# Top-k attention and a gated feed-forward on one core: the first two batches in another order, and one full product for the left-over keys

## The chip, the core and the metric

The kernel runs on one core of a Trainium2 chip. Time is device time in microseconds (us), the median over runs of the whole kernel. The engines are called PE (TensorE, matrix products; PEld is its weight load), DVE (VectorE), ACT (ScalarE), POOL (GpSimd) and SP (SyncE, which only issues transfers here).

## What is computed

The reference has two blocks, one behind the other, all in float32.

```python
# attention: q, k, v are (8, 8, 576, 64): batch, head, position, dimension
scores = scale * np.matmul(q, k.transpose(0, 1, 3, 2))
kth = np.partition(scores, -top_k, axis=-1)[..., -top_k:-top_k + 1]   # top_k = 32
scores = np.where(scores >= kth, scores, -1000000000.0)
scores = scores - np.max(scores, axis=-1, keepdims=True)
attn = np.exp(scores)
attn = attn / (np.sum(attn, axis=-1, keepdims=True) + 1e-09)
attn_out = np.matmul(attn, v)
# feed-forward on (4608, 512): one row per batch and position, heads side by side
h = x @ w_in                                  # w_in (512, 2048)
g = h * np.clip(h + 3.0, 0.0, 6.0) / 6.0
out = g @ w_out                               # w_out (2048, 512)
```

## The kernel before

**Tiles.** The 576 positions of a head are 4 tiles of 128 and a rest of 64. Two heads make a `Pair`, which is loaded, transposed on PE and kept for the whole batch. A `Duo` is two pairs (four heads) for one query tile `qt`; two duos cover a tile of a batch. A duo with `qt == J` (J is 4) is a left-over duo: its 64 remaining queries of both heads of a pair share the 128 partitions, so that it has half the rows to search. Each batch has eight full and two left-over duos, 80 in all.

**A duo's work, in order.** `scores` makes the products on PE, and ACT copies them from PSUM to `sc`. `top` finds the 32nd largest score of a row on DVE: four rounds of MAX8 (L249) with MATCH_REPLACE8 (L253) between them, for pair 0 and then for pair 1. `shift` (POOL, L262 and L265) and `exp` (ACT, L272 to L282) make the masked exponentials and their sum; `inverse` (DVE, L286) is the reciprocal; `weights` (POOL) scales the rows (L296) and splits the words into 16-bit halves (L305); `flip` (L311) transposes them by a transfer that SP issues; `join` puts the halves together again (L317), for pair 0 on ACT and for pair 1 on POOL. `values` multiplies by v on PE (L337) into one PSUM tile `pv`, and ACT copies this to the tokens `xT`, or `xr` for left-over queries (L344). In `values`, the two heads of a pair are side by side as two tiles of 64 columns of the array: four products of 128 keys each from `vm`, and a fifth from `vr` for the 64 left-over keys of each head. `vr` has zeros where the other head's keys are, and both heads' left-over weights lie in the same tile `eT[:, J, :]`.

**The written-out order.** There is no automatic scheduling. The main loop goes through the duos `m`, with eight slots `i` each; slot number 8m + i. In each slot come one round of `top`, then `convert_step`, then `parts(slot)`, which emits the steps of earlier duos that are due, then `piece`, which emits feed-forward work. The tables `usual`, `early` (duos 0 and 1) and `soon` (the last two) say how many slots after its duo's first slot a step is due: in `usual`, `exp0` at 4, `inverse0` at 7, `join0` at 13, `values` at 20. Each engine works off its instructions in the order in which they were emitted.

**Weights.** `w_in` and `w_out` arrive as 64-bit numbers and are converted in 32 chunks, one per slot in the first duos: a load (L102), Abs and a scaled copy on ACT (L108, L111) with a clamp on POOL (L109), then two DVE operations (L117, L118), then an add on POOL (L122). `convert` is a generator; before, it yields once after the load and once after the first stage, and DVE's part comes two slots after ACT's.

**Feed-forward.** `feed_forward` works on a block of 128 or 256 tokens: products `h` (L361), ACT's relu and copy, the gate on POOL (L375, L376), products `acc` (L383), a scaled copy and the output. A 128-token block is 16 pieces and a 256-token block 32. The main loop emits some 3 to 9 pieces a duo, by how many are left. Blocks have 256 tokens (`two`) in batches 1 to 6 and 128 in batches 0 and 7; the left-over queries of two batches make one 128-token block in `xr`, of which there is one buffer. `xT` has two, so `values` first emits all that is left of the block that last used the buffer:

```python
if hp == 0 and c0 == 0:
    while len(blocks) > 1 and blocks[-2] in todo:
        piece()
    state["xT"] = xtpool.tile([P, NHP, 2 * P], F32, tag="xT", name="xT")
```

Of the kernel before, what the change touches and what calls it, by code (L numbers as in the profile page):

```python
# [29 lines left out]
def kernel(  # L30
# [9 lines left out]
    nc = tc.nc  # L40
    P = nc.NUM_PARTITIONS
    B, H, S, D = q.shape
    DM, FF = moe_w_in.shape
    J = S // P
# [51 lines left out]
    def convert(dst, src):  # L96

        st = kqpool.tile([P, 2 * WC], U32, tag="kq", name="st")
        nc.sync.dma_start(st[:], src)  # L102
        yield
        words = st[:].rearrange("p (n two) -> p n two", two=2)
        lo, hi = words[:, :, 0], words[:, :, 1]
        a = gpool.tile([P, WC], F32, tag="g", name="a")
        y = gpool.tile([P, WC], F32, tag="g", name="y")
        nc.scalar.activation(a[:], hi.bitcast(F32), AF.Abs)  # L108
        nc.gpsimd.tensor_scalar(a[:], a[:], HI_MOST, HI_LEAST, ALU.min, ALU.max)  # L109

        nc.scalar.activation(y[:], lo, AF.Copy, bias=2.0, scale=2.0**-51)  # L111
        yield

        au, yu = a[:].bitcast(U32), y[:].bitcast(U32)
        nc.vector.tensor_scalar(au, au, 3, None, ALU.logical_shift_left)  # L117
        nc.vector.scalar_tensor_tensor(  # L118
            out=yu, in0=hi, scalar=0x80000000, in1=yu,
            op0=ALU.bitwise_and, op1=ALU.bitwise_or,  # L120
        )
        nc.gpsimd.tensor_tensor(  # L122
            dst.bitcast(I32), a[:].bitcast(I32), y[:].bitcast(I32), ALU.add
        )
# [59 lines left out]
    class Duo:  # L184
# [4 lines left out]


        def __init__(self, pairs, qt):
            self.pairs, self.qt = pairs, qt
            self.rest = qt == J
            self.nt = 1 if self.rest else 2
            self.nb = J + 2 if self.rest else 2 * J + 1
            self.m, self.less = [None] * 2, [None] * 2
            self.e16, self.t16, self.eT = [None] * 2, [None] * 2, [None] * 2
# [115 lines left out]
        def join(self, u):  # L313

            eT = self.eT[u] = kqpool.tile([P, 2 * J + 1, P], F32, tag="kq", name="eT")
            copy = nc.gpsimd.tensor_copy if u else nc.scalar.copy
            copy(  # L317
                eT[:, 0 : self.nb, :]
                .rearrange("p c q -> p (c q)")
                .bitcast(U16)  # L320
                .rearrange("p (x h) -> p h x", h=2),
                self.t16[u][:, 0 : 2 * self.nb, :].rearrange("p (h c) q -> p h (c q)", h=2),
            )

        def values(self, dst):

            w = R if self.rest else P
            pv = ps_w.tile([P, 512], F32, tag="w", name="pv")
            for u in range(2):
                pr, eT = self.pairs[u], self.eT[u]  # L330
                for c in range(J + 1):
                    for hh in range(2):
                        if self.rest:
                            rhs = eT[:, c if c < J else J + hh, hh * R : (hh + 1) * R]
                        else:
                            rhs = eT[:, c if hh == 0 or c == J else J + 1 + c, :]
                        nc.tensor.matmul(  # L337
                            pv[hh * D : (hh + 1) * D, u * w : (u + 1) * w],
                            pr.vm[:, hh, c, :] if c < J else pr.vr[:, hh, :],
                            rhs,  # L340
                            start=(c == 0),
                            stop=(c == J),
                        )
            nc.scalar.copy(dst, pv[:, 0 : 2 * w].rearrange("p (u q) -> p u q", u=2))  # L344


# [55 lines left out]
    duos = []  # L402
    for b in range(B):
        halves = [pairs[b][0:2], pairs[b][2:4]]
        for qt in range(J):
            duos += [Duo(h, qt) for h in halves]

            if b == B - 1 and qt == 0:
                duos += [Duo(h, J) for h in halves]
            elif b < B - 1 and qt % 2 == 0:  # L410
                duos.append(Duo(halves[qt // 2], J))
    assert J == NHP == 4
    per_batch = 2 * J + 2
    ND = len(duos)
    todo = []
    blocks = []
    left = 0
# [2 lines left out]
    def piece(count=1):  # L420
        nonlocal left
        for _ in range(count):
            while todo:
                try:
                    gates.append(next(todo[0]))
                    left -= 1
                    break
                except StopIteration:
                    todo.pop(0)
            else:  # L430
                gates.append(None)
            if len(gates) > 2:
                gate = gates.pop(0)
                if gate:
                    gate()

    def queue(*block):
        nonlocal left
        todo.append(feed_forward(*block))
        if block[0] is not state.get("xr"):  # L440
            blocks.append(todo[-1])
        left += block[1] // 8

    state = {}

    def values(m):

        u = duos[m]
        b, qt, hp = u.pairs[0].b, u.qt, u.pairs[0].hp
        if u.rest:  # L450
            if b % 2 == 0 and hp == 0:
                state["xr"] = xrpool.tile([P, NHP, P], F32, tag="xr", name="xr")
            u.values(state["xr"][:, hp : hp + 2, (b % 2) * R : (b % 2 + 1) * R])
            if b % 2 == 1 and hp == 2:

                def rows(t0):
                    return [
                        (i * R, (i + 1) * R, out[(b - 1 + i) * S + JP : (b + i) * S, :])
                        for i in range(2)
                    ]  # L460

                queue(state["xr"], P, rows)
            return

        two = 0 < b < B - 1
        c0 = qt % 2 * P if two else 0
        if hp == 0 and c0 == 0:
            while len(blocks) > 1 and blocks[-2] in todo:
                piece()
            state["xT"] = xtpool.tile([P, NHP, 2 * P], F32, tag="xT", name="xT")  # L470
        u.values(state["xT"][:, hp : hp + 2, c0 : c0 + P])
        if hp == 2 and (not two or c0):

            def rows(t0):
                t = qt - c0 // P + t0 // P
                return [(0, P, out[b * S + t : b * S + JP : J, :])]

            queue(state["xT"], c0 + P, rows)
# [8 lines left out]
            next(c)  # L487
            landing.append(c)

    def convert_step(depth=2):  # L490

        if len(converting) >= depth or not landing:
            for c in converting[:1]:
                next(c, None)
            del converting[:1]
        if landing:
            c = landing.pop(0)
            next(c)
            converting.append(c)
        land()  # L500

    def pair_at(m, first):
# [23 lines left out]
        shift1=7, exp1=8, inverse1=11, weights1=12, flip1=14, join1=17, values=20,  # L526
    )
    early = dict(
        shift0=3, exp0=3, inverse0=4, weights0=4, flip0=6, join0=8,
        shift1=7, exp1=7, inverse1=8, weights1=8, flip1=10, join1=12, values=13,  # L530
    )
    soon = dict(
        shift0=3, exp0=3, inverse0=5, weights0=5, flip0=7, join0=10,
# [4 lines left out]
        for part, at in (early if m < 2 else soon if m >= ND - 2 else usual).items():  # L538
            queued.setdefault(8 * m + at, []).append((m, part))

    def parts(slot):
        for m, part in sorted(queued.get(slot, []), key=lambda x: x[1][:-1] != "shift"):
            if part == "values":
                values(m)
            else:
                getattr(duos[m], part[:-1])(int(part[-1]))

    for m in range(ND + 3):
        u = duos[m] if m < ND else None

        level = (left >= 8) + (left >= 16) + (left >= 48)
        count = ((3, 4, 4, 5) if u and u.rest else (6, 7, 8, 9))[level]
        for i in range(8):
            if u:
                u.top(i // 4, i % 4)
            convert_step()
            if m == 0 and i == 0:
                first[3].load()
            if m == 0 and i in (1, 2):
                first[i + 1].transpose()  # L560
            if i == (3 if m == 0 else 1) and m + 1 < ND:
                duos[m + 1].scores()
            parts(8 * m + i)
            if m == 0 and i in (1, 4):
                for p in duos[i // 4].pairs:
                    p.load_values()
            if i == 0:
                p = pair_at(m, 4)
                if p:
                    p.load()  # L570
            if i == 3 and u and u.pairs[0].b and 1 <= m % per_batch <= 2:
                for p in duos[m - 1].pairs:
                    p.load_values()
            if i == 5:
                p = pair_at(m, 5)
                if p:
                    p.transpose()
            piece((i + 1) * count // 8 - i * count // 8)
# [36 lines left out]
```

## Time and profile before

| | before |
|---|---|
| median of 3 runs | 1631.08 us (1630.5 to 1633.21) |
| span of the profiled run | 1631.0 us |
| PE busy | 1466.9 us (90%) |
| DVE busy | 1470.0 us (90%) |
| ACT busy | 1088.6 us (67%) |
| POOL busy | 1140.9 us (70%) |
| MAX8 (L249), 1152 of them | 614.5 + 202.9 us on DVE |
| MATCH_REPLACE8 (L253), 864 of them | 423.8 + 211.9 us on DVE |
| feed-forward on PE (L361, L383) | 472.5 + 517.9 us |
| values on PE (L337) | 169.1 us with `vm`, 62.5 us with `vr` |

A busy time counts an engine only while an instruction runs on it. Each float32 product appears as two records of PE. In the profile's lines, an arrow points from what is read to what is written; "x16" is a count; square brackets at the end of a timeline row give how long the engine was idle ahead of it, and on whom it waited. The chain is followed back from the last instruction to whatever released each step, so that it says which engine set the pace at which time. The rows of 40 digits cut the span into equal slices, each digit being the busy share in tenths.

### The profile page before, as it was taken

Reading aid. Unit: us, or ns where it says so; the run is one execution under the profiler, and the core shown is the slowest. Engines: PE = TensorE matmul, PEld = TensorE weight load, DVE = VectorE, ACT = ScalarE, POOL = GpSimd, SP = SyncE. Lnnn points to the kernel's source line nnn. Section 1 sums busy time; section 2 is a strip of 40 time slices with the busy share of each in tenths; the row PEclk is TensorE's granted clock in tenths of the full one; section 3 lists DMA queues with packets and bytes.
Section 4 is the critical chain, followed back from the end, with each engine's and each line's share of the span. In section 5 each row is a group of like instructions: output and inputs, shape, how many; then the busy total and the mean of one; then the engine's idle time right before and its main releaser. Section 6 shows DMA issues by size and latency. Waiting matters only on the chain.

```text
span 1631.0 us, 25648 instructions
## 1 busy us (share of the span) xinstructions
PE 1466.9 (90%) x8736; PEld 979.2 (60%) x8736; DVE 1470.0 (90%) x3105; ACT 1088.6 (67%) x1863; POOL 1140.9 (70%) x1266
## 2 busy tenths in 40 slices
PE   5147699848999999899999999898999999899999
PEld 2134467627567584756567584656577584657775
DVE  5999999999999989999999889999999889999500
ACT  5566677667777676767767676767767676757521
POOL 3787577757787776867787776867787775867741
PEclk9568799979999999999999999999999999999999
DMA  8553434444444434454344424454354424333410
GB/s 231 156 171 64 101 63 89 97 95 83 71 98 99 94 56 92 86 109 85 65 104 89 94 56 92 88 107 84 65 105 89 94 56 94 80 60 72 66 22 13
DMA packets 450307, 144.29 MB, mean 88 GB/s; under 512 B 433280, under 2 KB 441472, under 8 KB 450176
## 3 DMA queue, kind: packets, MB, share of 16 engines
q1 hardware_dynamic: 450176, 142.65, 42.3%
q8 instruction: 69, 1.13, 0.3%
q14 instruction: 62, 0.51, 0.1%
HBM read 45.09 MB, written 9.44 MB: 33 GB/s over the span
## 4 chain that ended last, share of the span: by engine, by line
DVE 48%; PE 43%; ACT 3%; POOL 3%; SPq 1%; issue 1%; DMA 0%; POOLq 0%; ACTq 0%
DVE m L249 25%; DVE wk L253 20%; PE acc L383 16%; PE h L361 15%; PE pv L337 5%; PE big L226 3%; DVE y L118 1%; POOL eT L317 1%; PE big L229 1%; ACT sc L277 1%; DVE a L117 1%; SPq L150 1%; POOL sc L296 1%; PE big L214 1%; SPq L154 1%
## 5 line engine op out<-in xcount | busy, mean ns | idle before, releaser
L249 DVE MAX8 m<-wk 128x8 f32<-128x576 f32 x864 | 614.5, 748 | 3.1
L383 PE MATMUL acc<-w_out,g 128*128 128x512 f32 x1152 | 517.9, 600 | 5.1 <-POOL g L376 5.1
L361 PE MATMUL h<-xT,w_in 128*128 128x256 f32 (+1 forms) x2560 | 472.5, 343 | 0.0
L361 PEld LDWEIGHTS h<-xT,w_in 128*128 128x128 f32 x2560 | 410.0, 194 | 48.4 <-issue 10.3
L253 DVE MATCH_REPLACE8 wk<-m,wk 128x576 f32<-128x576 f32 x576 | 423.8, 742 | 0.0
L383 PEld LDWEIGHTS acc<-w_out,g 128*128 128x128 f32 x1152 | 213.5, 191 | 244.6 <-issue 234.6
L305 POOL COPY e<-sc 128x2304 uint16<-128x2304 uint16 (+1 forms) x192 | 322.0, 1687 | 10.1
L337 PE MATMUL pv<-eT,vm 128*64 128x128 f32 (+1 forms) x2560 | 169.1, 278 | 119.3 <-POOL eT L317 84.8
L272 ACT ACTIVATE sc<-sc,m 128x576 f32<-128x576 f32 x288 | 209.7, 773 | 47.5 <-DVE m L249 47.1
L337 PEld LDWEIGHTS pv<-eT,vm 128*64 128x64 f32 x2560 | 138.2, 144 | 161.7 <-POOL eT L317 89.6
L277 ACT ACTIVATE sc<-sc,shift 128x576 f32<-128x576 f32 x288 | 219.8, 766 | 21.5 <-POOL shift L265 18.7
L296 POOL TENSOR_SCALAR sc<-sc,den 128x576 f32<-128x576 f32 x288 | 213.0, 750 | 27.6 <-DVE den L286 27.1
L262 POOL TENSOR_TENSOR shift<-m 128x2 f32<-128x2 f32 (+1 forms) x160 | 32.1, 201 | 269.7 <-DVE den L286 266.8
L317 POOL COPY eT<-t 128x2304 uint16<-128x2304 uint16 (+1 forms) x80 | 208.5, 2606 | 5.7 <-DMA t<-e 4.6
L253 DVE MATCH_REPLACE8 wk<-m,sc 128x576 f32<-128x576 f32 x288 | 211.9, 742 | 0.0
L317 ACT COPY eT<-t 128x2304 uint16<-128x2304 uint16 (+1 forms) x80 | 208.9, 2611 | 0.0
L249 DVE MAX8 m<-sc 128x8 f32<-128x576 f32 x288 | 202.9, 741 | 0.9 <-ACT sc L235 0.9
L376 POOL TENSOR_TENSOR g<-g,hs 128x512 f32<-128x512 f32 x144 | 183.7, 1276 | 12.0
L344 ACT COPY xT<-pv 128x256 f32<-128x256 f32 x64 | 23.8, 372 | 232.8 <-PE pv L337 232.8
L375 POOL TENSOR_SCALAR g<-g 128x512 f32<-128x512 f32 x144 | 88.6, 615 | 95.3 <-ACT g L369 85.4
L226 PE MATMUL big<-kq 64*128 64x512 f32 x512 | 133.0, 638 | 10.3 <-ACT kr L182 10.3
L369 ACT ACTIVATE g<-h,three 128x512 f32<-128x512 f32 x144 | 98.4, 684 | 62.3 <-PE h L361 59.8
(47 smaller groups left out, 1210.4 us busy)
## 6 DMA issues: line engine op xcount, KB each, us to landing
landed<-in_k_dram SPq DMA_DIRECT2D x64, 128.0 KB, 3.0
landed<-in_q_dram SPq DMA_DIRECT2D x64, 128.0 KB, 2.9
st<-in_moe_w_in_dram SPq DMA_DIRECT2D x16, 512.0 KB, 5.0
vm<-in_v_dram SPq DMA_DIRECT2D x64, 128.0 KB, 2.3
st<-in_moe_w_out_dram SPq DMA_DIRECT2D x16, 512.0 KB, 3.8
out_dram<-o SPq DMA_DIRECT2D x32, 256.0 KB, 2.4
t<-e SPq DMA_TRANSPOSE x160, 4.6
landed<-in_k_dram SPq DMA_DIRECT2D x32, 32.0 KB, 2.6
```

Of the source, the lines that this page charges most:

```text
L226: nc.tensor.matmul(banks[:, 2 * i + hh, :], pr.qT[d, qs], pr.kT[d, :])
L249: nc.vector.max(self.m[u][:, t, 8 * r : 8 * r + 8], self.cur[t])
L253: nc.vector.match_replace(wk, self.m[u][:, t, 8 * r : 8 * r + 8], self.cur[t], LOWEST)
L272: nc.scalar.activation(row, row, AF.Prelu, bias=m[:, t, TOP_K - 1 : TOP_K], scale=-1.0, alpha=FLAT)
L277: nc.scalar.activation(row, row, AF.Exp, bias=self.less[u][:, t : t + 1], scale=-scale / FLAT, accum_out=self.den[:, u, t : t + 1],)
L296: nc.gpsimd.tensor_scalar(row, row, self.den[:, u, t : t + 1], 1.0, ALU.mult, ALU.mult)
L305: nc.gpsimd.tensor_copy(halves[:, :, to : to + c1 - c0], words)
L317: copy(eT[:, 0 : self.nb, :] .rearrange("p c q -> p (c q)") .bitcast(U16) .rearrange("p (x h) -> p h x", h=2), self.t16[u][:, 0 : 2 * self ...
L337: nc.tensor.matmul(pv[hh * D : (hh + 1) * D, u * w : (u + 1) * w], pr.vm[:, hh, c, :] if c < J else pr.vr[:, hh, :], rhs, start=(c == 0), ...
L361: nc.tensor.matmul(h[:, (f - f0) * nt : (f - f0 + 1) * nt], w_in[:, i, f * P : (f + 1) * P], xT[:, i, 0:nt], start=(i == 0), stop=(i == NH ...
L376: nc.gpsimd.tensor_tensor(g[:], g[:], hs[:], ALU.mult)
L383: nc.tensor.matmul(acc[:], gs[f // nf][:, c0 : c0 + P], w_out[:, f, :], start=(f == 0), stop=(f == NFC - 1),)
```

## The change

It has five parts. The duos of batches 0 and 1 come in another order: all eight full ones first, then both left-over ones (batch 7 has both behind its first tile, before and after; batches 2 to 6 stay as they were); batch 1's blocks become 128 tokens, so that a block is complete after two duos instead of four. The one `xr` buffer is then reused sooner, and a second guard, `while state.get("rest") in todo: piece()`, emits what is left of its block before the buffer is taken again. The steps of duos 0 and 1 are due sooner (`flip`, `join` and `values` in `early`), and their second join is done by ACT. During the first four duos `parts` is called twice a slot: all but `inverse` and `weights` ahead of `convert_step`, these two behind it; `convert` gets a third stage, and every chunk under way moves on by a stage in each slot, so that DVE's part comes one slot after ACT's. Last, in the values of full duos the two 64-column products for the left-over keys are replaced by one product over the whole array for both heads, behind all the side-by-side ones of both pairs; the accumulation of the PSUM bank is then started only once.

The purpose is that the feed-forward gets its first tokens earlier, and that PE has fewer products to do.

```diff
@@ convert
             op0=ALU.bitwise_and, op1=ALU.bitwise_or,
         )
+        yield
         nc.gpsimd.tensor_tensor(
@@ join
-            copy = nc.gpsimd.tensor_copy if u else nc.scalar.copy
+            copy = nc.gpsimd.tensor_copy if u and not self.early else nc.scalar.copy
@@ values of a duo
-                for c in range(J + 1):
+                for c in range(J + self.rest):
...
-                            start=(c == 0),
+                            start=(c == 0 and (u == 0 or self.rest)),
                             stop=(c == J),
                         )
+            if not self.rest:
+                for u in range(2):
+                    nc.tensor.matmul(
+                        pv[:, u * w : (u + 1) * w],
+                        self.pairs[u].vr[:].rearrange("p h d -> p (h d)"),
+                        self.eT[u][:, J, :],
+                        start=False,
+                        stop=(u == 1),
+                    )
@@ order of the duos
-            if b == B - 1 and qt == 0:
+            if qt == (0 if b == B - 1 else J - 1) and not 1 < b < B - 1:
                 duos += [Duo(h, J) for h in halves]
-            elif b < B - 1 and qt % 2 == 0:
+            elif 1 < b < B - 1 and qt % 2 == 0:
                 duos.append(Duo(halves[qt // 2], J))
@@ values(m)
             if b % 2 == 0 and hp == 0:
+                while state.get("rest") in todo:
+                    piece()
                 state["xr"] = xrpool.tile([P, NHP, P], F32, tag="xr", name="xr")
...
                 queue(state["xr"], P, rows)
+                state["rest"] = todo[-1]
...
-        two = 0 < b < B - 1
+        two = 1 < b < B - 1
@@ convert_step
-        if len(converting) >= depth or not landing:
-            for c in converting[:1]:
-                next(c, None)
-            del converting[:1]
+        begun = list(converting)
+        for c in begun:
+            if next(c, "done") == "done":
+                converting.remove(c)
@@ early
-        shift0=3, exp0=3, inverse0=4, weights0=4, flip0=6, join0=8,
-        shift1=7, exp1=7, inverse1=8, weights1=8, flip1=10, join1=12, values=13,
+        shift0=3, exp0=3, inverse0=4, weights0=4, flip0=5, join0=7,
+        shift1=7, exp1=7, inverse1=8, weights1=8, flip1=9, join1=11, values=11,
@@ main loop
+            if m < 4:
+                parts(8 * m + i, False)
             convert_step()
...
-            if i == (3 if m == 0 else 1) and m + 1 < ND:
+            if i == (4 if m == 0 else 1) and m + 1 < ND:
                 duos[m + 1].scores()
-            parts(8 * m + i)
+            if m < 4:
+                parts(8 * m + i, True)
+            else:
+                parts(8 * m + i)
```

More of the change, by code (lines that the diff above doesn't have):

```diff
@@ L191, in __init__ @@
         def __init__(self, pairs, qt):
-            self.pairs, self.qt = pairs, qt
+            self.pairs, self.qt, self.early = pairs, qt, False
             self.rest = qt == J
@@ L335, in values @@
                         else:
-                            rhs = eT[:, c if hh == 0 or c == J else J + 1 + c, :]
+                            rhs = eT[:, c if hh == 0 else J + 1 + c, :]
                         nc.tensor.matmul(
@@ L414 @@
     ND = len(duos)
+    for u in duos[:2]:
+        u.early = True
     todo = []
@@ L488, in land, with convert_step @@
             landing.append(c)
-    def convert_step(depth=2):
-        if len(converting) >= depth or not landing:
-            for c in converting[:1]:
-                next(c, None)
-            del converting[:1]
+    def convert_step():
+        begun = list(converting)
+        for c in begun:
+            if next(c, "done") == "done":
+                converting.remove(c)
         if landing:
@@ L539, with parts @@
             queued.setdefault(8 * m + at, []).append((m, part))
-    def parts(slot):
+    def parts(slot, late=None):
         for m, part in sorted(queued.get(slot, []), key=lambda x: x[1][:-1] != "shift"):
+            if late is not None and (part[:-1] in ("inverse", "weights")) != late:
+                continue
             if part == "values":
```

## The prediction

> **What bounds the kernel now.** I read the page first (busy shares, slices, chain), then the chain in order of time, then the VectorE rows with idle time ahead of them, then the neighbourhood of those rows on all engines.
>
> ```profile
> PE 1466.9 (90%) x8736; PEld 979.2 (60%) x8736; DVE 1470.0 (90%) x3105; ACT 1088.6 (67%) x1863; POOL 1140.9 (70%) x1266
> PE   5147699848999999899999999898999999899999
> DVE  5999999999999989999999889999999889999500
> DVE 48%; PE 43%; ACT 3%; POOL 3%; SPq 1%; issue 1%; DMA 0%; POOLq 0%; ACTq 0%
> ```
>
> Two engines are full. PE is underused in the first ten slices and VectorE (DVE) in the last three: this invites the thought that earlier tokens would fill PE and shorten its tail. The chain in order of time says when each of the two sets the pace:
>
> ```profile
> 137.32 1.65 DVE y L118
> 257.22 1.46 DVE wk L253 x2
> ...
> 656.28 2.10 POOL e L305
> 658.38 2.70 POOL eT L317
> 661.12 2.45 PE pv L337 x20
> ...
> 1389.96 2.10 POOL e L305
> 1392.20 2.70 POOL eT L317
> 1394.94 2.40 PE pv L337 x20
> 1397.35 5.25 PE h L361 x16
> ```
>
> Up to 445 us it is all DVE. Then stretches of PE alternate with DVE, and at 656 and 1390 (also at 745, 1023 and 1112) PE stood idle until a join (L317) of DVE's late products came: PE had no backlog there, whatever it had been late before. From 1395 on PE runs to the end. So the end is set by the moment at which DVE reaches about 1390, plus an in-order tail. DVE loses time only at these rows (and in batch 0, below):
>
> ```profile
> 40.70 0.17 DVE L286 RECIPROCAL den<-den 128x2 f32<-128x2 f32 x1 [7.93 <-ACT den L282]
> 576.48 0.16 DVE L286 RECIPROCAL den<-den 128x1 f32<-128x1 f32 x1 [5.93 <-ACT den L282]
> 943.42 0.16 DVE L286 RECIPROCAL den<-den 128x1 f32<-128x1 f32 x1 [10.02 <-ACT den L282]
> 1310.16 0.17 DVE L286 RECIPROCAL den<-den 128x1 f32<-128x1 f32 x1 [9.96 <-ACT den L282]
> 1413.29 0.16 DVE L286 RECIPROCAL den<-den 128x1 f32<-128x1 f32 x1 [1.82 <-ACT den L282]
> 1474.25 0.17 DVE L286 RECIPROCAL den<-den 128x2 f32<-128x2 f32 x1 [2.64 <-ACT den L282]
> ```
>
> The reader should see where the 5.9, 10.0, 10.0 and 2.6 come from: counting the loop, they fall on duos 27, 47, 67 and 76, where `while blocks[-2] in todo: piece()` emits 5, 7, 7 and 5 pieces of feed-forward at once. PE must finish them before the values; ScalarE (ACT) waits with the values' copy, the exponentials stand behind that copy, and the reciprocal behind them.
>
> **What the Trainium skill says.** "TensorE: Matmul & The Clock Gate", Part 2, has ACT, DVE and GpSimd (POOL) as strict FIFO queues; the four rows agree. "SBUF — State Buffer", Who interferes with whom: a two-port DVE operation and a GpSimd operation exclude each other for a whole instruction; the trace agrees (L118 took 2.58 us at 59.26 beside a POOL copy, 0.68 when alone). "TensorEngine Tiling (Array Packing)", Key Properties: changing the tiling mode drains the array. Before, values are entered and left once per duo; after, too, so no extra switch. "PSUM — Partial Sum Buffer" has a first matmul clear the written-bits of the whole bank: that explains the changed `start`, and costs nothing.
>
> **Part by part.**
>
> *Left-over product.* The 40 records of values take 2.33 us, in side-by-side pairs: 116 ns a pair. Two tiled pairs per tile, 0.233, become two full records of 112 ns (x128 of h at 14.29 us): 0.02 us less per tile. From 1395 on some 10 duos count: -0.3. If the switch costs more than before, say 0.1 a duo, +1.
>
> *Batch 1 in blocks of 128 tokens.* 512 records of 112 ns for 256 of 216: +2 us of PE, in a stage that DVE sets: 0.
>
> *Early tokens.* They reach PE earlier in batches 0 and 1, where PE waits for DVE: 0 by themselves. Counting pieces through both loops, what is left at each duo is the same from duo 48 on, and the order on every engine with it. So only DVE's arrival there counts.
>
> *Duo 24.* This is where the change pays. Batch 1's last left-over duo is now its tenth, its block is queued at slot 172, and duo 22's values (slot 196, in duo 24) must first drain it. Left at the start of duos 20 to 24: 25, 17, 25, 21, 13; emitted 8, 8, 4, 8, 3; so 10 remain and go at once: 2 x 1.79 (16 records of 112 ns) + 8 x 1.72 (4 of 429 ns) = 17.3 us. Before, in this place:
>
> ```profile
> 510.42 0.69 PE L337 MATMUL pv<-eT,vm 128*64 128x64 f32 x16
> 511.85 0.27 ACT L344 COPY xr<-pv 128x128 f32<-128x128 f32 x1 [1.89 <-PE pv L337]
> 515.00 0.20 ACT L282 ACTIVATE den<-den 128x2 f32<-128x2 f32 x1
> 520.31 0.15 DVE L286 RECIPROCAL den<-den 128x2 f32<-128x2 f32 x1
> ```
>
> PE would be one piece earlier (3 instead of 4 in this duo): 508.7 + 17.3 + 1.3 (values) + 0.3 (copy) + 3.3 (exponentials) = 530.9 against 520.3: DVE waits 10.6. Cross-check: 5 pieces in a full duo gave 2.64, so 10 give 2.64 + 5 x 1.73 = 11.3. Behind the waiting copy stand exponentials, score copies and joins; the reciprocal stops DVE's searches. Low bound 7, if PE arrives ahead. In return the drain at duo 27 goes: -5.9. At duo 47, 5 pieces instead of 7: -3.5 (2 x 1.73). Net +1.2.
>
> *Two left-over duos in a row.* Batches 0 and 1 now end like batch 7 begins. There the waits were 0.48, 0.23 and 1.82 = 2.5: the next values' join comes late against short duos. Twice 2.5, less 0.34 that batch 1 had: 4.7; I take 4, range 0 to 5.
>
> *Batch 0.* A full duo takes DVE 19.4 us (reciprocals 9.70 apart), a left-over one 11.35. 13.5 + 8 x 19.4 + 2 x 11.35 + 32 conversions of 1.03 = 224; the batch ended at 253.0. The excess of 29 is waits of 11.2 and conversions stretched by POOL. (Batch 1 took 178.4 against 177.9: nothing to gain.)
>  - Reciprocal of slot 4: the exponentials now stand ahead of the conversion and of duo 1's scores. ACT is free at 30.5; + 3.5 = 34.0; the chunk's Abs 0.67 and clamp 0.7 now follow, and DVE takes a chunk one slot later instead of two: 35.5, + 1.1 = 36.6, instead of 40.7: -4.1.
>  - Slot 8: from that reciprocal, scaling 1.5 + split copy 2.1 + flip 4.6 + join 2.8 + starts = 11.3; the join, now at slot 7, stands before the exponentials (3.4) on ACT; + 1.4 + 1.1 = 17.2, 18 with the slower split copy of 2.98. Before 15.35 (40.70 to 56.05): +2.3.
>  - Slot 12: join, values and their copy (2.9) all stand before duo 1's exponentials: 11.3 + 2.9 + 3.4 + 1.4 + 1.1 = 20.1; before 16.5: +3.6.
>  - Slot 16: 17.6 against 18.2 before: -0.6 (the joins of POOL that stretched conversions are ACT's now).
>  - Slots 17 to 31: before, seven of these were short left-over slots, too dense for POOL: 23.8 us for 17.2 of work, then 3.5 lost in duo 3. After, full slots: values of duo 1 cost some 2, three exponentials 0.9 each, stretch as in the first duos 0.4 x 12: 9.5 instead of 10.1: -0.6. One conversion is done earlier: -1.1.
>  Sum -0.5. Unknown: if the flips land in 6.5 (slowest in this stage) instead of 4.6, four waits grow by 1.9: +8; if the waits hide in stretches that are there anyway, -12.
>
> Sum: -0.3 + 1.2 + 4 - 0.5 = +4.4: **1635.5 us**.
>
> **Rivals.**
>  1. *Early tokens fill PE.* PE idled 135 us of the first 400; with blocks at half the grain one block (28 us) less is outstanding at slot 172. Were PE the bound from there, up to 20 us would come: 1611. Against: PE idle at 656, 745, 1023, 1112, 1390. Chance 0.06.
>  2. *Batch 0 is repaired.* The 7.9 wait and the dense left-over slots both go, joins cost nothing: -12 + 4 + 1.2 - 0.3 = -7, or -11 without the back-to-back waits: 1620 to 1625. For: both losses are in the trace and the edits aim at them. Against: joins and values stand ahead of exponentials. Chance 0.28.
>  3. *ACT becomes the bound of the first duos*, with flips slow behind weight loads: +8 + 4.4, 1643 to 1646. Chance 0.19.
>
> The forecast has 0.47, spread some 4 us around 1635.5.
>
> **How the numbers follow.** Slower by over 3.3 us: all of 3, and 0.33 of the forecast's 0.47: 0.52. Within: 0.12 of the forecast and 0.03 of rival 2: 0.15. Faster: the rest, 0.33. The range 1620 to 1647 holds the forecast, rival 3 and nearly all of 2; it leaves out rival 1 and some edges, under 0.2.
>
> **What would show it.** Right: a DVE wait of 7 to 12 at duo 24 (near 520), none at duo 27, one of 6 to 7 at duo 47, the same waits and emission from then on, PE's last stretch as long as before (1395 to its end). In batch 0, reciprocals near 36.6, 54, 75 and 93, waits for POOL's clamp ahead of L117. Wrong: batch 0 ends well before 253, no wait at duo 24 because PE came far ahead, or a tail of another length.

## The result and the profile after

The changed kernel takes **1647.97 us** (median of 4, 1647.83 to 1649.0) against 1631.5 us for the kernel before in the same runs: ratio 1.0101, 95% interval 1.0084 to 1.0119, so it is 1% slower. The profiled spans are 1647.2 and 1631.0 us, a difference of 16.2. The forecast was 1635.5 with a range up to 1647.0: right in sign, too small by 12.5, and the result lies 1 us above the range.

From the page of the changed kernel, the rows that answer to those of before: the busy shares, PE's and DVE's rows of slices, and the chain by engine.

```profile
PE 1476.9 (90%) x8736; PEld 995.9 (60%) x8736; DVE 1474.2 (89%) x3105; ACT 1092.6 (66%) x1865; POOL 1135.6 (69%) x1264
PE   5245889889999599898999999899999999899999
DVE  6899999999899899999999989999999989999600
PE 45%; DVE 41%; ACT 5%; POOL 4%; issue 2%; DMA 2%; SPq 1%; POOLq 0%; ACTq 0%
```

Busy time hardly moved: DVE has 4.2 us more, and 16 more of span. The early tokens are there (PE's slices 5 to 13 read 889889999 where they read 699848999 before), and yet the end came later. The chain in order of time (start, length, what) shows why that bought nothing:

```profile
672.43 1.90 issue
674.33 2.75 POOL eT L318
677.13 1.98 PE pv L338 x16
...
1405.52 2.10 POOL e L306
1407.77 2.69 POOL eT L318
1410.51 1.97 PE pv L338 x16
1413.63 5.11 PE h L371 x16
```

At 677 and 1410 PE again waited for a late join, as it had at 661 and 1395. The last stretch of PE starts some 16 us later and is as long as it was. So the whole loss lies ahead of it, in what DVE waits for. VectorE's timeline, the longer of its rows with idle time ahead (the bracket) from 240 to 1330 us:

```profile
252.02 0.16 DVE L287 RECIPROCAL den<-den 128x1 f32<-128x1 f32 x1 [1.16 <-ACT den L283]
260.04 0.16 DVE L287 RECIPROCAL den<-den 128x1 f32<-128x1 f32 x1 [2.24 <-ACT den L283]
434.55 0.16 DVE L287 RECIPROCAL den<-den 128x1 f32<-128x1 f32 x1 [2.16 <-ACT den L283]
442.28 0.17 DVE L287 RECIPROCAL den<-den 128x1 f32<-128x1 f32 x1 [1.96 <-ACT den L283]
542.34 0.17 DVE L287 RECIPROCAL den<-den 128x2 f32<-128x2 f32 x1 [10.99 <-ACT den L283]
682.57 0.16 DVE L287 RECIPROCAL den<-den 128x1 f32<-128x1 f32 x1 [1.02 <-ACT den L283]
957.38 0.17 DVE L287 RECIPROCAL den<-den 128x1 f32<-128x1 f32 x1 [6.75 <-ACT den L283]
1325.72 0.17 DVE L287 RECIPROCAL den<-den 128x1 f32<-128x1 f32 x1 [10.24 <-ACT den L283]
```

Not shown are 0.78 at 861, 1.01 at 1047 and 0.95 at 1226; the waits behind 1330 are nearly those of before. Each reciprocal marks how far DVE has come, so the offset between the same reciprocals in both traces, taken where both have the same work behind them, gives the loss by place. It adds up to the 16.2:

| place | offset gained, us | forecast, us |
|---|---|---|
| batch 0, without its two left-over duos | +3.65 | -0.5 |
| two left-over duos in a row, batches 0 and 1 | +7.2 | +4 |
| duo 24 / duo 27 / duo 47 | +11.1 / -6.0 / -3.3 | +10.6 / -5.9 / -3.5 |
| everything else: single left-over duos, duo 67, the tail | +3.5 | -0.3 |

The wait at duo 24 has the cause that was named. All engines near it: PE finishes the pieces of feed-forward that the guard emits at once (a drain, in what follows), then the left-over values, then ACT's copy, and only then the exponentials' sum and the reciprocal.

```profile
523.69 13.90 PE L393 MATMUL acc<-w_out,g 128*128 128x512 f32 x32
...
537.52 0.69 PE L338 MATMUL pv<-eT,vm 128*64 128x64 f32 x16
...
538.96 0.27 ACT L354 COPY xr<-pv 128x128 f32<-128x128 f32 x1 [0.73 <-PE pv L338]
542.10 0.20 ACT L283 ACTIVATE den<-den 128x2 f32<-128x2 f32 x1
542.34 0.17 DVE L287 RECIPROCAL den<-den 128x2 f32<-128x2 f32 x1 [10.99 <-ACT den L283]
```

In batch 0 the waits moved from the reciprocals to the conversions. All engines around slot 12:

```profile
64.60 2.77 ACT L318 COPY eT<-t 128x2304 uint16<-128x2304 uint16 x1 [5.77 <-DMA t<-e]
...
69.33 1.22 PE L347 MATMUL pv<-eT,vr 128*128 128x128 f32 x4
70.58 0.37 ACT L354 COPY xT<-pv 128x256 f32<-128x256 f32 x1 [3.21 <-PE pv L347]
70.85 1.44 ACT L273 ACTIVATE sc<-sc,m 128x576 f32<-128x576 f32 x2
...
73.95 0.64 ACT L108 ACTIVATE a<-st 128x512 f32<-128x512 f32 x1
74.68 0.61 POOL L109 TENSOR_SCALAR a<-a 128x512 f32<-128x512 f32 x1 [5.24 <-ACT a L108]
75.32 1.49 DVE L117 TENSOR_SCALAR a<-a 128x512 uint32<-128x512 uint32 x1 [4.70 <-POOL a L109]
```

ACT waits 5.77 us for a transpose, joins, waits 3.21 for the values, copies, makes the exponentials, and only then reaches the conversion's Abs (L108). POOL's clamp follows, and DVE, which has L117 next, has stood for 4.70 us.

### The profile page after: what moved, and what is told of

It reads as the page before. It is cut to its first block, busy times and chain, and to the rows that moved or that the text cites. A ratio compares the mean times of both kernels' runs of the same rounds, so it can differ in the third digit from the quotient of the medians.

```text
span 1647.2 us, 25650 instructions
## 1 busy us (share of the span) xinstructions
PE 1476.9 (90%) x8736; PEld 995.9 (60%) x8736; DVE 1474.2 (89%) x3105; ACT 1092.6 (66%) x1865; POOL 1135.6 (69%) x1264
## 4 chain that ended last, share of the span: by engine, by line
PE 45%; DVE 41%; ACT 5%; POOL 4%; issue 2%; DMA 2%; SPq 1%; POOLq 0%; ACTq 0%
DVE m L250 22%; DVE wk L254 18%; PE acc L393 16%; PE h L371 16%; PE pv L338 5%; PE big L227 4%; PE pv L347 2%; DMA t<-e 2%; ACT eT L318 1%; POOL eT L318 1%; ACT sc L278 1%; PE big L230 1%; POOL sc L297 1%; POOL e L306 1%; DVE y L118 1%
## 5 line engine op out<-in xcount | busy, mean ns | idle before, releaser
L371 PE MATMUL h<-xT,w_in 128*128 128x128 f32 (+1 forms) x2816 | 473.2, 327 | 0.0
L371 PEld LDWEIGHTS h<-xT,w_in 128*128 128x128 f32 x2816 | 422.1, 195 | 37.8 <-issue 5.7
L338 PE MATMUL pv<-eT,vm 128*64 128x128 f32 (+1 forms) x2560 | 162.8, 279 | 118.1 <-POOL eT L318 60.9
L263 POOL TENSOR_TENSOR shift<-m 128x2 f32<-128x2 f32 (+1 forms) x160 | 35.6, 222 | 298.7 <-DVE den L287 279.6
L318 ACT COPY eT<-t 128x2304 uint16<-128x2304 uint16 (+1 forms) x82 | 214.4, 2615 | 25.8 <-DMA t<-e 25.8
L318 POOL COPY eT<-t 128x2304 uint16<-128x2304 uint16 (+1 forms) x78 | 202.5, 2597 | 6.4 <-DMA t<-e 3.9
```

Of the source, the lines that this page charges most:

```text
L318: copy(eT[:, 0 : self.nb, :] .rearrange("p c q -> p (c q)") .bitcast(U16) .rearrange("p (x h) -> p h x", h=2), self.t16[u][:, 0 : 2 * self ...
L338: nc.tensor.matmul(pv[hh * D : (hh + 1) * D, u * w : (u + 1) * w], pr.vm[:, hh, c, :] if c < J else pr.vr[:, hh, :], rhs, start=(c == 0 an ...
L371: nc.tensor.matmul(h[:, (f - f0) * nt : (f - f0 + 1) * nt], w_in[:, i, f * P : (f + 1) * P], xT[:, i, 0:nt], start=(i == 0), stop=(i == NH ...
```

## The experiments

Theory A in what follows is the one that was kept: the end follows DVE; DVE loses time where the exponentials or the conversion stand behind something slower on ACT; each part of the change makes or takes such places. Other letters are the rivals, as each expectation describes them. Each run was timed beside the kernel before (medians 1631.87, 1632.1 and 1632.38 in three sets). What a part adds is read from the difference of medians, and from the offsets of the reciprocals.

**The product alone.** The kernel before, with the last part of the change only:

```diff
-                for c in range(J + 1):
+                for c in range(J + self.rest):
+            if not self.rest:
+                for u in range(2):
+                    nc.tensor.matmul(... vr of both heads, eT[:, J, :] ...)
```

> The kernel before with the full-array product alone. Theory A (VectorE sets the pace through what stands in ScalarE's queue; the product costs only where PE has idled and its clock is down, 0.7 us from the join to the end of the values' copy): the single left-over duos' waits grow from about 0.3 to 1.0 us each, some seven of them, so 1631.5 + 4 = 1635 to 1636, busy PE little changed. Theory B (PE sets the pace, the product costs 0.11 us in each of 64 duos): +7, 1638, with PE's part of the chain grown. Theory C (the product saves PE time, as forecast): 1631 or a little less.

It took 1636.04 us, ratio 1.0025 (1.0015 to 1.0036): 4 us slower, though the product replaces two records by one. The lines by shape (busy us, mean ns), of the kernel before and then of the changed one, say why it saves nothing:

```profile
L337 PE MATMUL pv<-eT,vr 128*64 128x128 f32 x512 | 53.2, 289 | 0.0
```

```profile
L347 PE MATMUL pv<-eT,vr 128*128 128x128 f32 x256 | 51.8, 331 | 0.0
```

Half the records, nearly the same PE time (51.2 us in this run): the two tiled ones had run side by side. And it costs latency where somebody waits. PE's and ACT's rows at the same left-over place, in the kernel before and then in the changed one:

```profile
661.12 1.97 PE L337 MATMUL pv<-eT,vm 128*64 128x128 f32 x16 [4.69 <-POOL eT L317]
662.88 0.64 PE L337 MATMUL pv<-eT,vr 128*64 128x128 f32 x4
663.59 0.37 ACT L344 COPY xT<-pv 128x256 f32<-128x256 f32 x1 [3.73 <-PE pv L337]
```

```profile
677.13 1.98 PE L338 MATMUL pv<-eT,vm 128*64 128x128 f32 x16 [5.28 <-POOL eT L318]
679.04 1.22 PE L347 MATMUL pv<-eT,vr 128*128 128x128 f32 x4
680.30 0.37 ACT L354 COPY xT<-pv 128x256 f32<-128x256 f32 x1 [4.43 <-PE pv L347]
```

From the first product to the copy: 2.47 before, 3.17 after, 0.70 more. The left-over product of the pair whose weights had come early used to be done by then; now it stands behind the late pair as well. And PE, after some 5 us of idleness, was slow. In the changed kernel, where PE had been busy:

```profile
731.40 0.71 PE L347 MATMUL pv<-eT,vr 128*128 128x128 f32 x4
```

The four records took 0.71 us there and 1.22 at 679. The granted clock was 1.00 from 729 to 732 us and 0.50 from 677 to 681. The Trainium skill says so ("TensorE: Matmul & The Clock Gate", Part 1, What's actually happening: the clock halves when the array has been idle); this clock agrees, and the records, whose ends are modelled, are longer by 1.7. The reciprocal behind this copy is then 0.68 later.

In this run's trace nine such places add 0.2 to 1.1 us each, 5.7 in all. The trace as a whole is only 2.7 us longer (1633.7 against 1631.0), because 1.4 is gained at the start, most of it ahead of the first values and so not by the product, and 1.5 at a few left-over duos from 1120 us on. Why these are shorter was not found. By the medians the product costs 4.2.

**The change with the tiled product again.** The same edit taken out of the changed kernel.

> The changed kernel with the left-over keys' products in two column tiles again. Theory A: the waits at the single left-over duos fall back from 1.0 to 0.3 us and the four at back-to-back left-over duos from 7.5 to about 5 in all: 1648 - 6 = 1642. Theory B: -7, over all stages. Theory C: 1649.

1640.15 us, ratio 1.0054 (1.0039 to 1.0069): 7.8 less than the change, and 8.7 less in the two profiled runs. By the reciprocals, 0.85 of it lies in the full duos of batch 0, 1.9 in the waits of left-over duos in a row (0.74, 2.05, 0.75, 2.05 instead of 1.16, 2.24, 2.16, 1.96), and the rest at later left-over duos: single ones, whose waits fell from up to 1.0 to some 0.34 or to nothing, and some 1.5 at the drains of duos 24, 47 and 67. So the product costs more in the new order (7.8) than in the old (4.2). Part of the difference is the four waits in a row, where the old order of batches 0 and 1 has a single place of this kind (0.68 in the run above), and the 0.85 of batch 0; the rest was not traced.

**A second buffer for the left-over tokens.** It takes the reason for the guard away:

```diff
-    xrpool = pool("xr", 1)
+    xrpool = pool("xr", 2)
-                while state.get("rest") in todo:
-                    piece()
```

> The changed kernel with two xr buffers and without the second guard, so that nothing is drained at duo 24. Theory A: VectorE's wait of 11.0 us at duo 24 goes, and none returns at duo 27 (by the count nothing is drained there): 1648 - 11 = 1637. Theory B (PE sets the pace): PE has the same work, so within 3 us of 1648.

1636.61 us, ratio 1.0028 (1.0016 to 1.0039): 11.4 less. VectorE's timeline around duo 24:

```profile
521.24 0.15 DVE L287 RECIPROCAL den<-den 128x2 f32<-128x2 f32 x1
530.94 0.15 DVE L287 RECIPROCAL den<-den 128x2 f32<-128x2 f32 x1
540.64 0.15 DVE L287 RECIPROCAL den<-den 128x2 f32<-128x2 f32 x1
```

They are 9.70 apart, the plain pace of a pair, and there is no bracket. Nothing of the 11 us came back later, at duo 27 or elsewhere. The largest single loss of the change is thus this one reuse of a buffer.

**Exponentials first in the first four duos.** If the joins ahead of the exponentials cost batch 0 its time, the other order should repair it:

```diff
-key=lambda x: x[1][:-1] != "shift"
+key=lambda x: ("shift", "exp").index(x[1][:-1]) if slot < 32 and x[1][:-1] in ("shift", "exp")
+    else 2 * (x[1][:-1] != "shift")
```

> The changed kernel with the exponentials of the first four duos emitted ahead of the joins and values of the same slot. Theory A: in slots 8, 12 and 16 VectorE no longer waits for exponentials behind joins (waits of 1.2, 4.7 and 1.1 us ahead of L117, and those that stretch them): batch 0 ends 4 to 7 us sooner, 1641 to 1644. Theory of early tokens (what counts is when the first values are there): the first values come 3.4 us later, so no gain or 3 us slower.

A miss: 1655.21 us, ratio 1.0145 (1.013 to 1.016), 7 us slower than the change and not faster. VectorE's timeline:

```profile
55.68 1.49 DVE L117 TENSOR_SCALAR a<-a 128x512 uint32<-128x512 uint32 x1 [3.37 <-POOL a L109]
...
79.69 1.49 DVE L117 TENSOR_SCALAR a<-a 128x512 uint32<-128x512 uint32 x1 [7.00 <-POOL a L109]
```

The waits grew from 1.23 to 3.37 and from 4.70 to 7.00. The exponentials of a slot need its last MAX8; the join doesn't, and could run while DVE still searched. Put behind the exponentials, it runs after them, and the conversion's Abs, which is behind both, comes later still. What DVE waits for in batch 0 is therefore the Abs, and the order of the two steps ahead of it mattered the other way round from what was expected.

**The conversion in its old stages.** The added `yield` taken out, and the old `convert_step(depth=2)` put back, in which DVE's part follows two slots after ACT's.

> The changed kernel with the conversions' stages as before (VectorE's part two slots after ScalarE's instead of one), all else changed. Theory A (VectorE is held in batch 0 by a chunk's Abs, which stands in ScalarE's queue behind join, values' copy and exponentials of its slot): the waits ahead of L117 in slots 8, 12, 16 and 20 (1.2, 4.7, 1.1, 1.6 us) go and only what the reciprocals then wait for remains, so 4 to 7 us less, 1641 to 1644. Theory B (it is held by the exponentials themselves, which stand behind the join): the same waits appear ahead of the reciprocals, 1646 to 1648.

1642.04 us, ratio 1.0061 (1.0046 to 1.0076), 5.9 less than the change, inside A's numbers. The place is not the one A gave. VectorE's timeline, the reciprocals of slots 4 and 12:

```profile
32.94 0.17 DVE L286 RECIPROCAL den<-den 128x2 f32<-128x2 f32 x1 [0.78 <-ACT den L282]
...
72.43 0.17 DVE L286 RECIPROCAL den<-den 128x2 f32<-128x2 f32 x1 [5.48 <-ACT den L282]
```

The gain of 4.9 is there at the first reciprocal (32.94 instead of 37.80), and then the waits come back, in front of the reciprocals and not of L117: 2.01 at slot 8, 5.48 at slot 12, 1.87 at slot 16. So it is the same delay on ACT in both; the stages decide only which DVE instruction meets it. One-slot stages cost DVE mainly before slot 4.

**The old order of duos and blocks.** With `two = 0 < b < B - 1` and one left-over duo behind every other tile:

> The changed kernel with the duos of batches 0 and 1 in the old order and batch 1 in blocks of 256; the first steps' schedule, the conversions and the product stay changed. Theory A: the four waits at back-to-back left-over duos (7.5 us) and the 11.0 at duo 24 go, about 6.6 at duo 27 and 10.3 at duo 47 come back: 1648 - 18.5 + 6.6 + 3.5 = 1640, if batch 0 costs what it costs now. Early tokens (they help, but something else eats the gain): 1648 or more, since the gain is taken away.

1643.04 us, ratio 1.0065 (1.0048 to 1.0082): 4.9 less, where A had 1640. As expected, there is no wait at duo 24, 6.56 is back at duo 27 and 10.24 at duo 47. But batch 0 then loses 7.0 instead of 3.65 (waits of 4.68, 2.33, 0.33 and 4.32 ahead of L117). Hence the new order does help batch 0, by some 3.4, and gives that and more back at its ends.

**The old early steps.** The first two duos' table as before, and the second join on POOL:

> The changed kernel with the steps of the first two duos due as before (flips at 6 and 10, joins at 8 and 12, values at 13, the second join on POOL). Theory A: join, values' copy and exponentials no longer meet in slot 11, so the wait of 4.7 us there goes and those of 1.2 and 1.1 at slots 7 and 15 shrink: 1642 to 1645. Early tokens: the first block is two slots (some 8 us) later, so 1648 or more.

1645.39 us, ratio 1.0078 (1.0063 to 1.0093): 2.6 less. At slot 12 the wait ahead of L117 fell from 4.70 to 0.48, but from L117's start to the reciprocal it then took 4.5 us instead of 2.4: L117 itself 2.94 instead of 1.49, beside POOL's join. Half of what the wait lost came back as longer instructions.

**Exponentials first throughout, on the kernel before.** If ACT's order turns a drain on PE into a wait of DVE, then it can be avoided without any part of the change:

```diff
-key=lambda x: x[1][:-1] != "shift"
+key=lambda x: ("shift", "exp").index(x[1][:-1]) if x[1][:-1] in ("shift", "exp") else 2
```

> The kernel before, with the exponentials emitted ahead of all other steps of the same slot but the shift, in the whole kernel: where a drain holds back the values' copy on ScalarE, the exponentials no longer stand behind it. Theory A: VectorE's waits of 5.9, 10.0 and 10.0 us at duos 27, 47 and 67 and the 1.8 and 2.6 at the end go, unless PE becomes the bound: 1606 to 1618. Theory B (PE sets the pace at the end, and its work is the same): 1628 to 1632.

1613.8 us, ratio 0.9889 (0.9874 to 0.9903). VectorE's timeline at duos 27, 47 and 67, which had 5.93, 10.02 and 9.96:

```profile
580.37 0.16 DVE L286 RECIPROCAL den<-den 128x1 f32<-128x1 f32 x1 [1.22 <-ACT den L282]
...
941.13 0.17 DVE L286 RECIPROCAL den<-den 128x1 f32<-128x1 f32 x1 [4.65 <-ACT den L282]
...
1301.93 0.16 DVE L286 RECIPROCAL den<-den 128x1 f32<-128x1 f32 x1 [4.66 <-ACT den L282]
```

ACT's copy of the values no longer stands between the last MAX8 and this duo's reciprocal, so the drain is met one reciprocal later (the one at 569.36, which waited before, is free now), and 4.7 to 5.4 us of each wait are gone.

**Then the second duo's scores one slot later** (`i == (4 if m == 0 else 1)`):

> The same, and the second duo's scores one slot later (as in the changed kernel), so that the first exponentials do not wait behind the scores' copy. Theory A: the wait of 7.9 us at the first reciprocal shrinks to 2 to 4: 4 to 6 us less than the run before it. Theory B: no difference to it.

1609.0 us, ratio 0.986 (0.9845 to 0.9874). The wait ahead of the first reciprocal is 2.01 (7.93 in the kernel before). On top of the exponentials, this one number of the change is worth some 5 us.

**The changed kernel with exponentials first from slot 32 on**, where no conversion of the first duos is left to suffer:

> The changed kernel with the exponentials ahead of the other steps of their slot from the fifth duo on (slot 32 and later); the drains stay, the order of PE's work too. Theory A (ScalarE's order turns a drain into a wait of VectorE): the wait of 11.0 at duo 24 shrinks to 1 to 2, that of 6.8 at duo 47 to 1 to 2, that of 10.2 at duo 67 to 5, those at left-over duos (7.5 back to back, 0.7 to 1.1 single) nearly go: 1648 - 28 to 33 = 1615 to 1620. Theory B (PE sets the pace): as the changed kernel, 1645 to 1648.

1621.92 us, ratio 0.9936 (0.9921 to 0.9951), 2 us above the expected range. The drain of duo 24 is met one reciprocal later, with 5.36 us of wait instead of 10.99, where 1 to 2 had been expected.

**This, with the tiled product and the old conversion:**

> That kernel, with the conversions' stages and the column-tiled product of before as well: what is left of the change is the order of batches 0 and 1, the blocks of 128 in batch 1 and the first two duos' schedule. Theory A: another 5 to 6 us from the conversions, 1 to 3 from the product (less than the 7.9 of its own run, since the waits that it lengthened are gone): 1607 to 1613. Early tokens (they help once VectorE is not held): below 1606.

1610.36 us, ratio 0.9862 (0.9846 to 0.9879), as A had it. It still has the new order of the duos and the early steps, and isn't faster than the 1609.0 above, which has neither.

**The fastest: the kernel before with exponentials first, the later scores, and batch 1 in blocks of 128 tokens** (`two = 1 < b < B - 1`):

> The fastest kernel so far (the one before with exponentials first and the second scores a slot later) with batch 1 in blocks of 128 alone, so that its first blocks are complete two duos after the start of the batch instead of four. Early tokens: with VectorE no longer held, PE's backlog matters and 5 us or more come: 1604 or less. Theory A: by the count the drain at duo 27 goes and that at duo 47 is 5 pieces instead of 7, worth 1.2 and 2 to 3, against 2 us more of PE's work: 1605 to 1608.

**1603.88 us** (1602.86 to 1605.3), ratio 0.9824 (0.9809 to 0.9839), faster than both kernels. The number is below what A expected and fits "early tokens"; the place doesn't. VectorE's timeline at duo 47, without the blocks and then with them:

```profile
936.37 0.16 DVE L286 RECIPROCAL den<-den 128x1 f32<-128x1 f32 x1 [5.39 <-ACT den L282]
```

```profile
930.58 0.16 DVE L286 RECIPROCAL den<-den 128x1 f32<-128x1 f32 x1 [1.23 <-ACT den L282]
```

Of the 5.8 us between these two rows, 0.2 was there at the first reciprocal, 1.5 came at duo 27, where a wait of 1.22 is gone, and 4.2 at duo 47; between the drains the two traces keep their distance to 0.2. At duo 47 the blocks have 256 tokens in both. It is the backlog that is lower, so that fewer pieces are left to be drained at once, as was counted for the change. Early tokens do fill PE (from 266 to 400 us it was busy for 124.7 us, against 104.6 without the blocks), but this pays later and elsewhere: at the drains that DVE waits for. Against the 1610.36 above, this kernel lacks the new order of the duos, the guard, the early steps and the divided `parts`, and has the exponentials first from the start; together these are worth 6.5 us.

## Why the prediction was wrong in size

The sum had +4.4, the traces 16.2. Of the 11.8 between them, 4.1 is batch 0, 3.8 the row "everything else", 3.2 the left-over duos in a row, and 0.6 the waits at duos 24, 27 and 47. The steps that failed are the cost of the product, which is in all three of the larger ones (without it, "everything else" would be -1.4 by the run with the tiled product), and the "+ 1.1" of batch 0.

**What held.** DVE's arrival sets the end and PE's tail keeps its length. The drain at duo 24 (10.6 forecast, 10.99 measured), the one that goes at duo 27 (-5.9, -6.0) and the smaller one at duo 47 (-3.5, -3.3) were counted right, from the pieces left in the loop. Together they are +1.2 forecast, +1.8 measured. Early tokens by themselves brought no shorter end, as the idle PE ahead of late joins had said (the chain up to 445 us is not quite all DVE, though: at 296 it passes through such a join, and below 90 through exponentials on ACT); what they brought is the drain that goes at duo 27 and the smaller one at duo 47.

**The left-over product, -0.3: the step that failed.** It was costed as PE time, in which it is indeed neutral, and the sentence "so no extra switch" overlooked where the switch now lies. "TensorEngine Tiling (Array Packing)", Key Properties, was read for how often the array drains, which no run here shows apart. The number of switches is the same, but the one back to the full array used to come behind the values and now stands inside them, ahead of ACT's copy, together with both pairs' left-over keys and at the clock of a PE that has just been idle. Measured: 0.70 us at the place shown, 4.2 us on the kernel before, 7.8 in the change. How the 0.70 divides between the array's drain, the order of the two pairs and the clock was not separated.

**Two left-over duos in a row, +4: too small.** Batch 7's waits were taken over (2.5 a batch); measured 3.4 and 4.1, less the 0.34 that batch 1 had before: 7.2. Some 1.9 of the 3.2 too little is the product, as the run without it shows (5.6 remain). What the other 1.3 comes from stays open; batch 7 differs in what else ACT does there, and that was not tried.

**Batch 0, -0.5: the waits were foreseen, the length of one instruction wasn't.** Slot 4 came at 37.80 (36.6 forecast), slot 8 at 56.05 (54), slot 12 at 77.75 (75), slot 16 at 95.84 (93; the terms themselves add up to 91.9, so that 3.9 was missing by then); slots 17 to 31 then gained 1.5 (1.7). The step that failed is "+ 1.1", the chunk's two DVE operations ahead of each of these reciprocals. They took 2.4 at all four (from 35.38 to 37.80, from 75.32 to 77.75). Of the 1.3 too little, some 1.1 is L117, 1.49 long instead of 0.41, and the rest L118, 1.09 instead of 0.68. Four times 1.3 is 5.2; the other terms of these slots were too long and took back 1.3. POOL's timeline at slot 12:

```profile
74.68 0.61 POOL L109 TENSOR_SCALAR a<-a 128x512 f32<-128x512 f32 x1 [5.24 <-ACT a L108]
75.25 1.27 POOL L123 TENSOR_TENSOR w_in<-a,y 128x512 int32<-128x512 int32 x1
```

With the added `yield`, the add of the chunk before (L123) is emitted behind this chunk's clamp (L109). The clamp releases L117, and at the same time POOL begins the add, which lasts until 76.52; L117 ends just behind it. The same pair of rows is there at 34.73. By shape, the lines of before and after:

```profile
L117 DVE TENSOR_SCALAR a<-a 128x512 uint32<-128x512 uint32 x32 | 23.3, 727 | 10.8 <-POOL a L109 10.8
```

```profile
L117 DVE TENSOR_SCALAR a<-a 128x512 uint32<-128x512 uint32 x32 | 27.1, 846 | 22.3 <-POOL a L109 22.3
```

3.8 us more of busy time is about what batch 0 lost. The wait only moved: 11.5 more is here, and the 11.2 ahead of batch 0's first four reciprocals are gone. The prediction credited the new stages with an earlier conversion and put no price on the third. The run with the old conversion agrees in size: it took 5.9 less, and L117 was busy for 21.1 us in it, 6.0 less. A run with the third stage alone removed was not made, so that POOL's order as the cause is read from the trace and not tested apart. The product adds 0.85 to batch 0.

One reference of the prediction is off, not what it rests on: the Trainium skill has the strict queues of "TensorE: Matmul & The Clock Gate" in Part 1, Architectural detail, and not in Part 2.

**The range** ended at 1647 because its upper case was slow transposes. In batch 0 they landed in 4.6 to 4.7 us, as in the forecast's main case. What carried the time there was three small terms of one sign: 4 in batch 0, 3 in the rows of left-over duos, 4 for the product elsewhere. The spread of some 4 us around the sum left no room for three such errors at once, and the product is in all three.

## What to carry to other kernels

On an engine that works in order, ask of each instruction that waits what stands behind it: here a copy of values ahead of exponentials turned PE's backlog into idle VectorE, and one changed sort key gave 1.1%. Cost an edit at the place where somebody waits for it, at the clock and in the order that hold there, not by its share of busy time: a product that was neutral in PE time cost 4 to 8 us as latency. Before reusing a buffer sooner, count what is left of its readers' work at that moment; the guard of one small buffer cost 11 us, and a second buffer took it away.

## What the runs showed of the hardware

- Four full-array records of 128x128 float32 took 0.71 us on a busy PE and 1.22 after some 5 us of idleness (granted clock 1.00 and 0.50); four column-tiled ones for one pair took 0.39 and 0.64.
- L117 alone took 0.40 to 0.43 us, beside POOL's add 1.49, and beside POOL's join 2.94. That an instruction of this kind can be held for the whole length of POOL's agrees with the Trainium skill, "SBUF — State Buffer", Who interferes with whom. What had not been expected is how regularly it happens: at all seven places of the changed kernel at which DVE waited for the clamp and an add stood behind it, L117 took 1.48 to 1.50.
